# Attention with normed q and k, then a gelu MLP: the first two batches' steps issued in another order

## Chip, cores and metric

The kernel runs on one core of a Trainium2 chip. The metric is the device time of one execution in microseconds (us); the time given for a kernel is the median of its runs. The engines have in-order queues of their own: TensorE (PE; its weight loads are PEld), VectorE (DVE), ScalarE (ACT), GpSimd (POOL) and SyncE (SP, which only issues DMAs). Waits between them are semaphores, put in from the data that each instruction reads and writes.

## What is computed

Eight batches of attention with twelve heads, 448 tokens and a head size of 64, with q and k normed by their root mean square, and then two matrix products with a gelu between, on all 3584 tokens.

```python
def rmsnorm(x, g):
    rms = np.sqrt(np.mean(x * x, axis=-1, keepdims=True) + 1e-06)
    return x / rms * g
q_n, k_n = (rmsnorm(q, g_q), rmsnorm(k, g_k))
scores = scale * np.matmul(q_n, k_n.transpose(0, 1, 3, 2))
scores = scores - np.max(scores, axis=-1, keepdims=True)
attn = np.exp(scores)
attn = attn / (np.sum(attn, axis=-1, keepdims=True) + 1e-09)
x = np.matmul(attn, v)                 # heads side by side: 3584 x 768
h = x @ w_in                           # 768 x 2048
g = 0.5 * h * (1.0 + np.tanh(c * (h + 0.044715 * h * h * h)))
out = g @ w_out                        # 2048 x 768
```

## The kernel before

A batch is handled in three chunks of four heads (`c` = 0, 1, 2). The step names below carry an operand, a batch and a chunk: `q01` is q of batch 0, chunk 1. For each chunk of q and k the kernel loads the raw rows, squares them, totals the squares over the head (a row sum), takes the inverse root, multiplies (the norm), turns the result so that the head dimension lies on partitions, and puts it into `qT` or `kT`. The gains of q and k are multiplied into one column that scales `kT`. A constant `shift`, bounded from the gains, stands in for the row maximum in the exponential.

A *unit* (L325) is one seventh of a chunk's keys: TensorE makes scores in a pair of PSUM banks, ScalarE writes their exponentials to `ex`. There are 21 units in a batch, seven for each chunk. *Sums* are products of `ex` with ones (the softmax denominators), *products* are those with v. The denominators are transposed (`st`), inverted and spread (`rb`), and the products times `rb` are `xT`, the input of the MLP. The first layer (`hh` or a PSUM pair, L599) gives gelu's input, ScalarE writes `g`. The second layer takes two batches' tokens in quarters (L443): one *step* is four small matmuls, 32 steps make a group, and the group's last step copies its PSUM pair to `osb`. The second layer of batch 0 has 96 steps, which are mixed with the attention of batch 1.

Schedules are in the order of issue (`tc.manual_schedule()`): nothing reorders them. For batches 0 and 1 that order is a string, read by `first_two` (L814). From the first layer of batch 1 on, the loop over batches sets it. The words of the string:

- `y`, `z`, `w`: filler matmuls of zeros on TensorE (L272), 168 columns wide (`y`) or 448; `y` and `z` write the bank of `o`, `w` a buffer of the PSUM pool `ps_m`, which has two, taken in turn by turned tiles, roots, the sums of chunk 2 and `hh`. A number behind repeats the word.
- `L.q10`: a load of raw q or k on SP's queue (L125). The buffers rotate in fours, so a load waits for the square and the norm that read the buffer last.
- `sq`, `to`, `nm`, `tu`, `pu`: square (L170, L172), total (L177), norm (L279), turn (L297) and put (L306 to L310). `.A`, `.V`, `.P` name ScalarE, VectorE or GpSimd, `.h0`, `.h1` half the heads, `.t0`, `.t1` four and three of the seven token groups.
- `rA`, `rB`, `rC`, `r1`, `r2`, `rE`: inverse roots on ScalarE, a logarithm and exponentials (L202 to L221); `N1`: those of batch 1 by Newton steps on VectorE (L231 to L246). `eG`, `eE` load ScalarE's table for gelu or exp.
- `gp`, `gc`, `gm`, `sh`: the gains' product on GpSimd (L766), its transpose on VectorE (L772), the bound on TensorE (L777) and the shift on VectorE (L780, L784).
- `VV`, `Y`, `W`, `OO`: loads on GpSimd's DMA queue: v of a batch (L148, 672 KB as written), the first half of the columns of `win` in six parts (L738, 256 KB; `Y.10` is chunk 1, part 0), the second half in four (L728, 384 KB), and `wout` in two (L745, 1536 KB).
- `U`: a unit. `A`: an addition of exponentials on VectorE, which shortens the sums of batch 1. `s.c`, `x.c`: sums and products of a chunk, with a range of units behind. `t`, `r`, `q.c`: transpose of the denominators (L392), inverse and spread (L400, L401), and `xT` (L409, L415), all on VectorE.
- `m.i`: the first layer for a pair of column blocks (`e` the four parts of `xT` from chunks 0 and 1, `l` the last two), `h` half of one. `m.2.e` is the first, into `hh`.
- `a`, `d`: one second-layer step; the letter says whether ScalarE (`a`) or VectorE (`d`) makes the copy, and has an effect in the last step of a group alone.
- `dt`, `gn`: a transposing DMA on SP's queue (L315) in place of turn and put, and the gain for it. `PS`, `PT`: batch 1 begins; the small PSUM pools become two more pairs. `rel`: frees the spare raw buffers.

A sum or product of chunk `c` writes the same two banks `o` as the one before, so `x.0` waits for `t`, and `s.1` for `q.0`. The middle step of each second-layer group also puts a wait into SP's queue (L452).

Of the kernel before, what the change touches and what calls it, by code (L numbers as in the profile page):

```python
# [17 lines left out]
def kernel(  # L18
# [39 lines left out]
    gp = ctx.enter_context(tc.tile_pool(name="gp", bufs=1))  # L58
# [755 lines left out]
    def first_two(steps, m2):  # L814
# [3 lines left out]
        for step in steps.split():  # L818
# [78 lines left out]
            else:  # L897
# [10 lines left out]
                 "eE": lambda: nc.scalar.preload_act_table_set(EXP_SET)}[kind]()  # L908

    m2 = []  # L910
    first_two((
# [24 lines left out]
            )    , m2)  # L936
    begun = 2
    quads = ((3, 4), (5, 6))
    for b in range(1, B):
# [86 lines left out]
```

## Time and profile before

| | |
|---|---|
| Time, median of 3 runs | 393.82 us (393.76 to 394.06) |
| The profiled execution | 394.05 us, of which the span of the trace is 392.1 |
| TensorE busy | 384.0 us |
| ScalarE busy | 277.8 us |
| VectorE busy | 271.9 us |
| GpSimd busy | 125.8 us |
| DMA | 54.36 MB in 65770 packets |

Times in the profile count from the start of the span. A line of a timeline has start, length, engine, line, operation, what it writes and reads by the program's names, the shape, the count, and in brackets the engine's idle time before it with what ended that. Neighbouring instructions of one kind are merged. TensorE's matmuls overlap, and their ends are modelled. A DMA's landing is told as the time from its issue.

### The profile page before, as it was taken

The page shows a single profiled execution, that of the slowest core. Times are in us where ns is not written, and L with a number is a line of the kernel's source. Part 1 is how long each engine was busy: PE and PEld are TensorE (multiplying, and loading weights), DVE is VectorE, ACT ScalarE, POOL GpSimd, SP SyncE. Part 2 cuts the span into 40 slices and gives each one's busy share as a digit, 9 for nine tenths or more (in the row PEclk, how much of TensorE's full clock was granted, in tenths as well). Part 3 has the DMA queues.
Part 4 walks back from the last instruction along what each step waited for, and adds up shares of the span by engine and source line. Part 5 has one row for each costly group of instructions (what it writes and reads, how often), then busy time and mean ns, then how long its engine had stood idle before and what let it go on. Part 6 is the DMA issues. An engine that isn't in the chain of part 4 may idle for free.

```text
span 392.1 us, 12742 instructions
## 1 busy us (share of the span) xinstructions
PE 384.0 (98%) x5649; PEld 245.3 (63%) x5649; DVE 271.9 (69%) x424; ACT 277.8 (71%) x349; POOL 125.8 (32%) x105
## 2 busy tenths in 40 slices
PE   7989999999999999999999999999999999999996
PEld 6455567855676558865666557865566556875554
DVE  4999539996699357963599456982579613999743
ACT  6995489567996589857898479857899349873410
POOL 5995501863304540083301840054400900000000
PEclk9999999999999999999999999999999999999999
DMA  8999997899752969249651859239632621120024
GB/s 266 255 233 222 204 186 153 303 185 260 150 135 56 249 81 225 55 98 272 106 144 42 192 137 205 65 86 230 118 75 46 132 47 43 43 57 27 0 61 101
DMA packets 65770, 54.36 MB, mean 139 GB/s; under 512 B 37428, under 2 KB 60852, under 8 KB 65716
## 3 DMA queue, kind: packets, MB, share of 16 engines
q1 hardware_dynamic: 53200, 41.33, 41.9%
q0 software_dynamic: 12128, 11.80, 19.4%
q8 instruction: 44, 0.72, 0.8%
q10 hardware_dynamic: 388, 0.43, 0.3%
q14 instruction: 10, 0.08, 0.1%
HBM read 45.61 MB, written 11.01 MB: 144 GB/s over the span
## 4 chain that ended last, share of the span: by engine, by line
PE 91%; ACT 5%; DVE 1%; DMA 1%; issue 0%; POOL 0%; ACTq 0%
PE s L599 21%; PE t L443 19%; PE t L599 15%; PE s L443 12%; PE s L383 6%; ACT ex L338 4%; PE s L334 4%; PE t L334 3%; PE t L383 3%; PE s L529 2%; PE t L529 2%; PE o L383 1%; PE tp L297 1%; DMA rawq<-in_q_dram 1%; PE hh L599 1%
## 5 line engine op out<-in xcount | busy, mean ns | idle before, releaser
L599 PEld LDWEIGHTS <-win 128*128 128x128 bf16 x768 | 74.4, 98 | 70.8 <-issue 2.6
L443 PEld LDWEIGHTS <-g 64*64 64x64 bf16 x3072 | 98.0, 107 | 32.8 <-SPq L452 2.9
L338 ACT ACTIVATE ex<-s,shift 128x896 bf16<-128x896 f32 x101 | 97.8, 1011 | 4.5 <-PE s L334 2.7
L443 PE MATMUL t<-wout,g 64*64 64x384 bf16 x1792 | 90.4, 323 | 0.0
L599 PE MATMUL s<-xT,win 128*128 128x448 bf16 x438 | 88.3, 353 | 0.0
L177 DVE TENSOR_REDUCE ss<-sq 128x14 f32<-128x896 f32 (+3 forms) x45 | 44.4, 997 | 48.1 <-ACT sq L170 42.9
L338 ACT ACTIVATE ex<-t,shift 128x896 bf16<-128x896 f32 x67 | 66.4, 1014 | 5.8 <-PE t L334 3.0
L612 ACT ACTIVATE g<-s 128x896 bf16<-128x896 f32 (+1 forms) x41 | 34.0, 835 | 48.5 <-PE s L599 48.5
L599 PE MATMUL t<-xT,win 128*128 128x448 bf16 x318 | 64.7, 353 | 0.0
L443 PE MATMUL s<-wout,g 64*64 64x384 bf16 x1280 | 64.6, 323 | 0.1
L612 ACT ACTIVATE g<-t 128x896 bf16<-128x896 f32 (+1 forms) x30 | 24.8, 829 | 26.3 <-PE t L599 26.3
L334 PE MATMUL s<-qT,kT 64*64 64x448 bf16 x404 | 37.6, 353 | 2.0 <-ACT ex L338 1.5
L756 POOL COPY mark<-es 1x1 bf16<-1x1 bf16 x5 | 0.9, 177 | 116.0 <-DVE es L357 116.0
L279 POOL TENSOR_TENSOR nrmk<-rawk,rinv 128x896 bf16<-128x896 f32 (+1 forms) x21 | 34.5, 1647 | 5.4 <-DVE o L246 5.4
L279 POOL TENSOR_TENSOR nrmq<-rawq,rinv 128x896 bf16<-128x896 f32 (+1 forms) x21 | 34.5, 1643 | 4.2 <-ACT rinv L209 2.9
L334 PEld LDWEIGHTS <-kT 64*64 64x64 bf16 x672 | 23.7, 106 | 14.7 <-issue 6.3
L172 POOL TENSOR_TENSOR sq<-rawq 128x896 f32<-128x896 f32 (+1 forms) x9 | 13.6, 1516 | 54.1 <-DVE ss L177 28.2
L383 PEld LDWEIGHTS <-vb 64*64 64x64 bf16 x672 | 22.9, 107 | 8.1 <-issue 0.3
L401 DVE STREAM_TRANSPOSE rb<-rc 128x896 f32<-128x896 f32 x24 | 26.7, 1112 | 0.8
L334 PE MATMUL t<-qT,kT 64*64 64x448 bf16 x268 | 24.1, 351 | 0.3 <-ACT ex L338 0.2
L360 DVE TENSOR_TENSOR e<-ex 128x896 bf16<-128x896 bf16 x33 | 20.0, 606 | 6.2 <-ACT ex L338 6.2
L383 PE MATMUL s<-ex,vb 64*64 64x448 bf16 x420 | 22.8, 349 | 0.0
(123 smaller groups left out, 404.2 us busy)
## 6 DMA issues: line engine op xcount, KB each, us to landing
rawk<-in_k_dram SPq DMA_DIRECT2D x23, 448.0 KB, 5.6
out_dram<-osb SPq DMA_DIRECT2D x52, 192.0 KB, 3.1
rawq<-in_q_dram SPq DMA_DIRECT2D x22, 448.0 KB, 4.8
vb<-in_v_dram POOLq DMA_DIRECT2D x8, 672.0 KB, 7.2
wout<-in_moe_w_out_dram POOLq DMA_DIRECT2D x2, 1536.0 KB, 23.4
win<-in_moe_w_in_dram POOLq DMA_DIRECT2D x6, 256.0 KB, 11.2
win<-in_moe_w_in_dram POOLq DMA_DIRECT2D x4, 384.0 KB, 13.4
rawq<-in_q_dram SPq DMA_DIRECT2D x3, 224.0 KB, 3.9
```

Source lines behind the costliest of these rows:

```text
L172: eng.tensor_mul(sq, raw, raw)
L177: nc.vector.reduce_sum(sss[b][:, c, "qk".index(n), hs, ts], squares(b, c, n, hs, ts), axis=AX.X)
L279: eng.tensor_mul(nrms[n, b, c][:, ts].rearrange("p t a d -> p a t d"), raws[n, b, c][:, :, ts], root[:, :, ts].to_broadcast([P, 2, m, D]),)
L334: nc.tensor.matmul(sc[r * R:(r + 1) * R, a, :S], kT[rs, c, t, r], qT[b][rs, c, :, r], start=True, stop=True,)
L338: nc.scalar.activation(ex[:, t], sc[:, :, :S], AF.Exp, scale=scale, bias=shift)
L360: nc.vector.tensor_add(e2, ex[:, t - 1], ex[:, t])
L383: nc.tensor.matmul(o[r][a * D:(a + 1) * D], vb[b % 2][rs, 2 * c + a, i] if what else ones[rs], es[i][rs, a], start=(i == 0), stop=(i == n ...
L401: nc.vector.transpose(rb.rearrange("p r s -> p (r s)"), rc.to_broadcast([128, 2 * S // 32, 32]))
L443: done = nc.tensor.matmul(o[c * R:(c + 1) * R, n, :HD], g[rs, f, i * 128 + c * R:i * 128 + (c + 1) * R], wout[rs, f, half * HD:(half + 1) ...
L529: nc.tensor.matmul(o[:, lo:hi], g_of(qd, m, f), w_of(m, f)[:, lo:hi], start=start and f == 0, stop=f == nh - 1, skip_group_check=True,)
L599: nc.tensor.matmul(h[j][:, :S] if type(h) is list else h[:, j, :S], win[:, c, f * 128:(f + 1) * 128], xT[b][:, c], start=(c == 0), stop=(c ...
L612: nc.scalar.activation(g[:, 2 * i + lo:2 * i + js[-1] + 1, (b % 2) * S:(b % 2 + 1) * S], h[:, lo:js[-1] + 1, :S], AF.Gelu_apprx_tanh)
```

## The change

Only the string is changed: the same steps, but for two things, in another order. Sixteen of the 96 second-layer steps have the letter `a` instead of `d`, and the square `sq.k21.h1` is ScalarE's instead of GpSimd's. Of the fillers, `z1` stands ahead of the 48 `y`, and `z6`, `w5` and two single `z` stand ahead of or among the turns of `q00`; formerly `w5` and most `z` stood among the units of chunk 0. `gp` stands ahead of the first GpSimd norm. On GpSimd's DMA queue the order was `VV.0`, `Y.00`, `Y.01`, `Y.10`, `Y.11`, `Y.20`, `Y.21`, `W.10` to `W.13`, `OO.0`, `OO.1`, `VV.1`; it is now `VV.0`, `W.13`, `Y.11`, `Y.01`, `Y.21`, `Y.00`, `Y.10`, `Y.20`, `W.12`, `W.11`, `W.10`, `VV.1`, `OO.0`, `OO.1`. `nm.k01.P.t1` stands ahead of `sq.k02.P`. In batch 1 units, steps, additions, loads, squares and totals are mixed in another way.

```diff
--- before.py
+++ after.py
@@ -908,32 +908,24 @@
                  "eE": lambda: nc.scalar.preload_act_table_set(EXP_SET)}[kind]()
 
     m2 = []
-    first_two((
-                "y48 sq.q00.A.h0 to.q00.h0 sq.q00.A.h1 z3 to.q00.h1 sq.k00.A.t0 "
-                "to.k00.t0 sq.k00.P.t1 rA nm.q00.P.t1 gp rB nm.q00.V.t0 L.q10 "
-                "sq.q01.A tu.q00.t0 tu.q00.t1 nm.k00.V.t0 pu.q00.A VV.0 gc z1 "
-                "to.k00.t1 rC tu.k00.t0 pu.k00.V.t0 gm sh z1 U2 nm.k00.V.t1 w5 "
-                "sq.k01.P sq.k02.P tu.k00.t1 to.q01 to.k01 U r1 sq.q02.P U "
-                "pu.k00.V.t1 nm.k01.V.t0 z1 nm.q01.V to.q02 z6 U z1 U to.k02 s.0.01 "
-                "U s.0.13 nm.k01.P.t1 tu.q01 s.0.34 pu.q01.V tu.k01 Y.00 Y.01 Y.10 "
-                "r2 s.0.47 pu.k01.V.t0 U L.k10 U Y.11 Y.20 nm.q02.P Y.21 t sq.q10.P "
-                "sq.k10.P W.10 W.11 nm.k02.V.t0 nm.k02.V.t1 W.12 W.13 pu.k01.V.t1 "
-                "z4 z1 r U x.0.01 L.q12 sq.q12.P x.0.12 OO.0 x.0.23 OO.1 rel U "
-                "tu.q02 tu.k02 pu.k02.V.t1 pu.k02.V.t0 U pu.q02.V x.0.37 q.0 to.q10 "
-                "L.k12 L.q11 to.k10 U3 s.1.05 VV.1 U s.1.57 U2 t s.2.01 x.1.03 U "
-                "x.1.35 U x.1.57 r q.1 U eG s.2.16 x.2.01 sq.k12.P x.2.13 to.q12 "
-                "s.2.67 x.2.37 t r q.2 to.k12 sq.q11.A L.k11 m.2.e sq.k11.P to.q11 "
-                "to.k11 N1 nm.k11.P nm.k12.P m.0.e m.1.e m.0.l m.1.l nm.q12.P "
-                "nm.q10.V nm.k10.V m.2.l m.3 m.4 nm.q11.V tu.q10 pu.q10.V m.5 "
-                "tu.k10 m.6 tu.q11 pu.q11.V pu.k10.V h.7.0 h.7.1 PS a eE tu.k11 "
-                "pu.k11.V U A PT a6 U a3 U2 a2 d4 dt.k12 d dt.q12 U2 d7 A U A3 d U "
-                "d A2 d U d9 A U d4 a s.0 A U A t r a6 d L.q20 L.k20 L.q21 gn.12 U2 "
-                "A2 U A L.k21 sq.q20.P sq.k20.P d sq.q21.P.h0 sq.k21.P.h0 L.q22 "
-                "L.k22 sq.q21.P.h1 d4 x.0 U A U d5 q.0 s.1 t d2 A2 U2 d2 "
-                "sq.k21.P.h1 d3 A d to.k20 d5 U2 r to.q21.h0 to.q20 x.1 U a d a "
-                "to.k21.h0 A2 q.1 A to.q21.h1 L.q30 L.k30 a2 x.2 a4 A s.2 sq.q22.A "
-                "sq.k22.P t d9 r d2 to.k21.h1 rE d2 VV.2 d2 a eG q.2 m.0.e m.1.e"
-            )    , m2)
+    first_two(("z1 y48 sq.q00.A.h0 sq.k00.P.t1 z3 to.q00.h0 gp sq.q00.A.h1 to.q00.h1 sq.k00.A.t0 to.k00.t0 rA "
+               "z6 nm.q00.V.t0 rB nm.k00.V.t0 w5 sq.q01.A tu.q00.t0 z1 z1 nm.q00.P.t1 tu.q00.t1 pu.q00.A "
+               "to.k00.t1 tu.k00.t0 L.q10 VV.0 gc rC z1 pu.k00.V.t0 gm sh to.q01 U2 nm.k00.V.t1 sq.k01.P W.13 U "
+               "to.k01 r1 U tu.k00.t1 pu.k00.V.t1 nm.k01.V.t0 U2 nm.q01.V sq.q02.P nm.k01.P.t1 tu.k01 sq.k02.P "
+               "U Y.11 to.q02 Y.01 s.0.01 tu.q01 Y.21 s.0.13 s.0.34 pu.k01.V.t0 to.k02 s.0.47 r2 nm.q02.P "
+               "pu.q01.V U2 t Y.00 L.k10 sq.q10.P sq.k10.P Y.10 nm.k02.V.t1 Y.20 z1 nm.k02.V.t0 W.12 z4 W.11 "
+               "pu.k01.V.t1 r U W.10 x.0.01 VV.1 x.0.12 x.0.23 U L.q12 tu.k02 pu.k02.V.t1 tu.q02 U pu.q02.V "
+               "pu.k02.V.t0 x.0.37 U sq.q12.P U2 q.0 s.1.05 OO.0 to.q10 U s.1.57 U to.k10 U t s.2.01 x.1.03 U "
+               "x.1.35 x.1.57 U L.k12 sq.k12.P r U eG L.k11 q.1 rel s.2.16 OO.1 x.2.01 x.2.13 L.q11 to.q12 "
+               "s.2.67 x.2.37 t sq.k11.P r q.2 m.2.e m.0.e sq.q11.A to.q11 to.k11 to.k12 N1 nm.q10.V nm.k10.V "
+               "m.1.e m.0.l m.1.l m.2.l m.3 m.4 tu.q10 nm.q12.P m.5 m.6 tu.k10 pu.k10.V h.7.0 h.7.1 PS d "
+               "pu.q10.V eE nm.q11.V tu.q11 nm.k11.P tu.k11 pu.q11.V U pu.k11.V PT d a A a3 U dt.q12 a d2 U2 d "
+               "a d2 nm.k12.P d a d U2 d A dt.k12 a d a A U d2 A a A d A2 a3 U a L.q20 A U a2 d3 a2 d a U d3 a2 "
+               "U A s.0 t a2 d U d A L.q21 a A L.k20 sq.k20.P d U gn.12 A2 U a A L.k21 L.k22 d L.q22 "
+               "sq.k21.P.h0 d2 L.q30 sq.q21.P.h0 r x.0 U a d U q.0 a d a3 s.1 a2 d t a sq.q20.P A2 U d2 A r a "
+               "sq.k21.A.h1 d2 U to.k20 a d4 U2 a A2 sq.q22.A d2 A d U to.q21.h0 L.k30 A a3 x.1 q.1 to.k21.h1 d "
+               "x.2 s.2 to.k21.h0 VV.2 t d a to.q20 d8 a sq.q21.P.h1 to.q21.h1 a d a sq.k22.P rE eG a r q.2 "
+               "m.0.e m.1.e"), m2)
     begun = 2
     quads = ((3, 4), (5, 6))
     for b in range(1, B):
```

## Prediction

> **What bounds the kernel now.** I read the page first, then stretches of the span, then each engine's timeline up to 36 us.
>
> ```profile
> span 392.1 us, 12742 instructions
> PE 384.0 (98%) x5649; PEld 245.3 (63%) x5649; DVE 271.9 (69%) x424; ACT 277.8 (71%) x349; POOL 125.8 (32%) x105
> ```
>
> TensorE is busy for 98% of the span, but part of that is filler (`y`, `z`, `w`: products of zeros). The next view gives busy time by stretch: PE, PEld, DVE, ACT, POOL, then clock and DMA.
>
> ```profile
> 9.88:31.17 21.29, 19.28 (x277) 10.41 (x274) 19.98 (x31) 20.42 (x27) 19.98 (x22) 1.00 1.08 245
> 32.30:52.00 19.70, 19.70 (x125) 10.60 (x121) 13.61 (x26) 8.07 (x12) 8.20 (x5) 1.00 1.26 206
> 52.00:80.00 28.00, 27.61 (x604) 20.67 (x601) 22.08 (x35) 22.03 (x24) 9.47 (x8) 1.00 0.91 204
> ```
>
> From 9.88 to 31.17 us ScalarE works 20.42 of 21.29 us: it leaves 0.87 us. From 32.30 to 80, past the end of what the change reorders, TensorE has no gap but 0.4 us between 52 and 80. So whatever batch 0's front loses or wins by 32.3 us is passed on whole, and behind it there is 0.4 us to win. ScalarE's timeline of the front:
>
> ```profile
> 7.65 0.95 ACT L170 ACTIVATE g<-rawq 128x896 f32<-128x896 f32 x1 [0.49 <-DMA rawq<-in_q_dram]
> 8.51 0.89 ACT L308 COPY qT<-tp 128x896 bf16<-128x896 bf16 x1
> 9.88 2.80 ACT L338 ACTIVATE ex<-s,shift 128x896 bf16<-128x896 f32 x3
> 13.15 3.68 ACT L338 ACTIVATE ex<-s,shift 128x896 bf16<-128x896 f32 x4
> 17.45 0.18 ACT L221 ACTIVATE root<-lg 128x14 f32<-128x14 f32 x1 [0.27 <-DVE qT L310]
> 18.23 12.92 ACT L338 ACTIVATE ex<-s,shift 128x896 bf16<-128x896 f32 x14 [0.47 <-PE s L334]
> ```
>
> The 21 exponentials (3, 4, 14) run nearly back to back, 12.92/14 = 0.92 us each. So the front's end is set by when the first begins, 9.88 us. That needs `qT` (8.51 + 0.89 = 9.40), the first scores, and the shift. TensorE up to there, and where the second layer's first half-batch begins:
>
> ```profile
> 1.17 5.79 PE L272 MATMUL o<-zeros 128*128 128x168 bf16 x51 [1.17 <-DVE zeros L84]
> 7.45 0.56 PE L297 MATMUL tp<-ident,nrmq 128*128 128x128 bf16 x7 [0.49 <-DVE nrmq L279]
> 8.37 0.41 PE L777 MATMUL s<-gprod,rows 32*128 32x32 f32 x4
> 9.44 0.57 PE L334 MATMUL s<-qT,kT 64*64 64x448 bf16 x8 [0.36 <-DVE shift L784]
> 9.95 1.12 PE L272 MATMUL w<-zeros 128*128 128x448 bf16 x5
> 12.15 1.50 PE L272 MATMUL o<-zeros 128*128 128x448 bf16 x7
> 32.32 1.68 PE L599 MATMUL hh<-xT,win 128*128 128x448 bf16 x8
> ```
>
> Ends are modelled; the next matmul issues before them. A `z` or `w` costs (1.50 - 1.12)/2 = 0.19 us of issue, and the last one's tail is 1.12 - 5 x 0.19 = 0.17. The opening filler (48 `y`, 3 `z`) issues until 6.96 - 0.17 = 6.80 us (rounded); after its end TensorE waits 0.49 us for the normed q. Its own slack ahead of the first turn is about half a microsecond.
>
> **The change, part by part.**
>
> *Fillers, the largest term.* Their number stays (48 `y`, 18 `z`, 5 `w`), but ahead of `tu.q00.t0` now stand one more `z` at the very front, `z6` and `w5`; two more split the seven turns. The first writes the `o` bank that holds nothing yet, `w` a fresh PSUM buffer, so neither waits; TensorE takes them in order. Eleven cost 11 x 0.19 = 2.09 us. The front `z` runs while TensorE is slow:
>
> ```profile
> 1.10:4.37 3.27, 3.20 (x24) 1.00 0.77 231
> 4.37:6.20 1.83, 1.83 (x27) 1.00 0.98 249
> ```
>
> Of the `y`, 24 fall in the first 3.27 us (0.14 each), 27 touch the next 1.83 (0.07 each), though the granted-clock column says 1.00 in both. If the slow stretch lasts a fixed time, the `z` pushes `y` into the fast part and costs 0.19 in the end; if a fixed number of matmuls, 0.14 x 448/168 = 0.37. I take the smaller, since the matmuls on both sides of the step are alike and only time has passed. [...] This trace alone fits both.
>
> So the first turn issues at 6.80 + 2.28 = 9.08 us instead of 7.45; seven turns to their end 0.56, two `z` between 0.38: done at 10.02. `pu.q00.A` starts at about 10.07 instead of 8.51: **+1.56 us**. In the old order it also waited for `sq.q01.A` to end, so 1.56 is what is left of TensorE's longer delay.
>
> *The gain product.* `gp` moves ahead of `nm.q00.P.t1` on POOL.
>
> ```profile
> 6.68 0.83 POOL L279 TENSOR_TENSOR nrmq<-rawq,rinv 128x384 bf16<-128x384 f32 x1 [0.18 <-ACT s L221]
> 7.47 0.57 POOL L766 TENSOR_TENSOR gprod<-grow 64x32 f32<-64x32 f32 x2
> ```
>
> ```profile
> 9.27 0.15 DVE L784 TENSOR_SCALAR shift<-shift 128x1 f32<-128x1 f32 x1
> ```
>
> The norm waits for the product's 0.57 less the 0.18 that POOL idled: it ends 0.4 later, near 7.9 us, covered by the fillers, which run to 9.08. Without that cover it would cost 0.4. The bound (`gm`) comes behind the turns of `q00` and half of `k00` and one `z` and ends near 10.75; the shift ended 0.64 behind it before (8.78 to 9.42), so by 11.4 at the latest. The first scores issue at 10.96 + 0.04 = 11.0 and the first exponential starts at 11.44, again +1.56, with the shift just in time.
>
> *Totals and norms of chunks 1 and 2.* `to.q01` now stands ahead of `nm.k00.V.t1`; it fills VectorE's wait of 0.41 us for the root of `rC` and delays `tu.k00.t1`, which only unit 5 needs, by then behind two exponentials: nothing. The root step `r1` is still between exponentials 3 and 4. Ahead of `r2` stands `pu.k01.V.t0` (0.48, below), which moves the root, bound to `pu.q01.V`, by 0.4; exponential 8 formerly waited for that same `kT`, and now for `pu.q01.V`: about equal. I take 0.1, bounds 0 and 0.5.
>
> ```profile
> 9.84 0.56 DVE L279 TENSOR_TENSOR nrmk<-rawk,o 128x384 bf16<-128x384 f32 x1 [0.41 <-ACT o L221]
> 16.74 0.61 DVE L310 COPY qT<-tp 128x896 bf16<-128x896 bf16 x1
> 17.27 0.48 DVE L306 TENSOR_SCALAR kT<-tp,gcols 128x512 bf16<-128x512 bf16 x1
> ```
>
> Units, sums and products of batch 0 keep their order but for one pair; each waits for the same releases 1.6 us later. `m.2.e` thus starts at 32.32 + 1.6 to 1.7 = 34.0.
>
> *POOL and the weight loads.* `nm.k01.P.t1` now stands ahead of `sq.k02.P`, so that square waits for the roots of `r1`, which ScalarE ends as it takes up exponential 4 (13.15 before, 14.7 now). Behind it are six of the ten loads of `win`; only `W.13` is issued early (10.6 us).
>
> ```profile
> 20.71 1.70 POOL L172 TENSOR_TENSOR sq<-rawq 128x896 f32<-128x896 f32 x1
> ```
>
> ```profile
> L738 POOL DMA_DIRECT2D win<-in_moe_w_in_dram x1: 642/642/642, 20.1 to 20.1; - x1
> ...
> DMA to landing us min/median/max: 13.3/13.3/13.3
> ```
>
> ```profile
> L728 POOL DMA_DIRECT2D win<-in_moe_w_in_dram x1: 665/665/665, 24.0 to 24.0; - x1
> ...
> DMA to landing us min/median/max: 11.6/11.6/11.6
> ```
>
> Adding POOL's durations (1.7 a square or norm, 0.64 an issue), `Y.11` is issued at 17.3 instead of `Y.00` at 15.4, and `Y.10`, the last part `m.2.e` needs, at 25.4. The queue lands parts in order: six of 256 KB by 20.1 + 13.3 = 33.4 us, the seventh, of 384 KB, by 35.6. `Y.10` now has `W.13` (384) and four `Y` ahead, with itself 1664 KB against 1536 and 1920: 33.4 + 2.2 x 128/384 = 34.1. The third matmul needs it at 34.4. No wait on this estimate; it can cost 1.2 if it lands like the seventh part. I take 0.1. `W.10` to `W.12` land as late as the old last part, under 43 us, when `m.4` comes. `OO.0` landed at 28.1 + 20.3 = 48.4 (below) and now lies behind `VV.1` too, 672 KB, at 2.2 us for 384 KB 3.8 us: there by 52.2, needed at 51.74 + 1.6 = 53.3, covered by 1.1.
>
> ```profile
> L745 POOL DMA_DIRECT2D wout<-in_moe_w_out_dram x1: 1211/1211/1211, 28.1 to 28.1; - x1
> ...
> DMA to landing us min/median/max: 20.3/20.3/20.3
> ```
>
> ```profile
> 51.74 0.36 PE L443 MATMUL s<-wout,g 64*64 64x384 bf16 x4
> ```
>
> SP's loads of batch 1 keep their order but for `k11` ahead of `q11`, and go 1.5 to 2 us later as their buffers come free; `to.q11` to `to.k12` wait for `q.2` anyway.
>
> *Batch 1.* Sixteen `d` become `a`. Only steps 32, 64 and 96 copy anything, and these are `d`, `d`, `a` before and after: nothing. `sq.k21.h1` moves from POOL to ScalarE, about half a square, in a stretch where ScalarE idles (22.03 of 28): nothing; uncovered 0.6. Two tiles are now turned behind `h.7` instead of one, which adds no work; but VectorE must do `pu.k10.V`, `pu.q10.V` and `nm.q11.V` (0.68 + 0.62 + 1.08 = 2.4 us) while TensorE does `h.7` (2.3 us of issue) and one step: 0.1, bounds 0 and 0.3.
>
> ```profile
> 43.66 1.08 DVE L279 TENSOR_TENSOR nrmq<-rawq,o 128x896 bf16<-128x896 f32 x1
> 50.12 0.68 DVE L306 TENSOR_SCALAR kT<-tp,gcols 128x896 bf16<-128x896 bf16 x1
> ```
>
> ```profile
> 49.38 2.43 PE L599 MATMUL s<-xT,win 128*128 128x448 bf16 x12
> ```
>
> Units stand with fewer steps between them at first (the sixth behind 16 steps, formerly 17), more later. The gap of 0.4 in 52 to 80 may go or double: 0, bounds -0.4 and +0.5. The loads of batch 2 leave earlier, and `dt.q12` no longer stands behind SP's wait for step 16.
>
> **Sum.** 1.56 + 0.1 + 0.1 + 0.1 + 0 = 1.9 us. The profiled execution took 394.05 us (span 392.1 and 1.95 around it), 0.23 above the median 393.82. So 394.05 + 1.86 = 395.9, and as a median **395.7 us**.
>
> **Rivals.**
>
> *The weights come late.* POOL's queue slides by more than counted and `Y.10` lands with the old seventh part or later. For it: DMA share 1.08 in the front. Against: the same bytes lie ahead within 128 KB. +1.2: 396.9.
>
> *TensorE slows again.* The `w5` at 9.95 us and the seven `z` at 12.15 are gone from a thin stretch; from 11 to 16.5 us TensorE would work under half the time. If it falls to its opening pace until rewarmed (3.2 us at half), 1.6 us of work is lost, partly in its 2.0 us of gaps: +1.2, 396.9. Against: no pause there exceeds 1 us. [...]
>
> *Batch 1 stalls.* Pairs of PSUM run short where units stand close: one exponential's length, 0.92 + 0.1: 396.7.
>
> *Not slower.* The fillers ahead of the first turn would have to fit into TensorE's 0.49 us there, that is cost 0.045 each, not 0.19. Then `pu.q00.A` stays at 8.51 behind `sq.q01.A`, the front keeps its times, and at best batch 1 wins its 0.4: 393.82 - 0.4 = 393.4. The turning point is `pu.q00.A` at 8.5. ScalarE can't win it back otherwise: its whole slack is 0.87, less than 1.56.
>
> **How the numbers follow.** Forecast 0.60 (394.9 to 396.4), late weights 0.13, slow TensorE 0.08, batch 1 stalls 0.10, not slower 0.09. The range 394.8 to 397.2 takes in all but the last and the tails. A measurement can tell about 0.2% (0.8 us) from no change: faster 0.06, same 0.04, slower 0.90.
>
> **What would show it.** Right: eleven fillers ahead of the first turn, that turn near 9.1 us, `pu.q00.A` at 10.1, first exponential at 11.4, `hh` at 34.0, no wait in TensorE from there to 54. Wrong: the first exponential before 10.5; `hh` over 34.5, with a wait for `win`; transposes at 0.11 instead of 0.055 apart around 16 us; gaps of TensorE over 0.9 us between 54 and 82.

## Result and the profile after

| | before | changed |
|---|---|---|
| Time, median of 6 runs each, side by side | 393.94 us (393.69 to 395.29) | 397.84 us (396.64 to 399.18) |
| Ratio | | 1.0092, 95% interval 1.0067 to 1.0117 |
| Profiled execution | 394.05 us, span 392.1 | 399.18 us, span 397.4 |

Slower, as forecast, but by 3.9 us and not by 1.9. Ratios, here and below, compare runs taken side by side and leave out the slow ones (two of the ten of fillers_back, one of the ten of shorter_opening), so a ratio need not be the quotient of two medians. The page of the changed kernel:

```profile
span 397.4 us, 12737 instructions
PE 385.7 (97%) x5649; PEld 246.9 (62%) x5649; DVE 274.2 (69%) x424; ACT 278.6 (70%) x350; POOL 125.0 (31%) x104
```

Stretches of the changed kernel: stretch, its length, busy time of PE, PEld, DVE, ACT, POOL, then TensorE's granted clock and DMA. The first two are the opening, the next three single out the clock, the last three answer to those shown of before:

```profile
1.10:4.37 3.27, 3.20 (x22) 2.98 (x23) 0.29 (x6) 1.76 (x2) 1.26 (x3) 1.00 0.75 245
4.37:7.24 2.87, 2.87 (x24) 2.87 (x22) 2.64 (x5) 2.12 (x8) 1.74 (x4) 1.00 0.97 303
10.65:14.03 3.38, 2.22 (x29) 1.40 (x27) 2.36 (x6) 2.56 (x5) 2.40 (x3) 1.00 1.18 228
14.03:17.44 3.41, 1.57 (x20) 0.58 (x16) 2.79 (x4) 3.38 (x7) 1.24 (x2) 1.00 1.17 215
17.44:20.85 3.41, 3.41 (x37) 1.94 (x38) 3.26 (x5) 2.75 (x5) 3.01 (x4) 0.50 0.85 250
12.75:34.00 21.25, 16.58 (x244) 9.44 (x243) 19.32 (x31) 19.60 (x27) 17.33 (x19) 0.92 1.07 230
36.19:55.22 19.03, 19.03 (x113) 10.07 (x110) 13.00 (x25) 7.90 (x11) 6.92 (x5) 1.00 1.27 202
55.22:83.95 28.73, 27.86 (x611) 20.94 (x611) 22.74 (x36) 22.50 (x25) 7.02 (x7) 1.00 0.91 203
```

Two things are new. From 4.37 to 7.24 us TensorE issues 24 matmuls in 2.87 us (0.12 each), the slow pace; in the profile of before the fast pace began near 4.4. The trace's own record of the clock begins only there, at 4.47 us before and at 7.20 in the changed kernel; ahead of it there is no entry, and the column shows 1.00. And from 17.44 to 20.85 the granted clock is 0.50, behind a stretch in which TensorE was busy 1.57 of 3.41 us. In before it was busy nearly throughout there, and the clock stayed up:

```profile
11.30:14.71 3.41, 3.13 (x26) 1.07 (x22) 2.97 (x5) 3.38 (x7) 3.34 (x3) 1.00 1.20 208
14.71:18.12 3.41, 3.28 (x54) 1.70 (x51) 3.27 (x6) 2.76 (x6) 3.41 (x6) 1.00 1.05 273
```

ScalarE's timeline of the changed kernel:

```profile
7.73 0.95 ACT L170 ACTIVATE g<-rawq 128x896 f32<-128x896 f32 x1 [0.95 <-DMA rawq<-in_q_dram]
11.36 0.91 ACT L308 COPY qT<-tp 128x896 bf16<-128x896 bf16 x1 [2.68 <-PE tp L297]
12.75 2.80 ACT L338 ACTIVATE ex<-s,shift 128x896 bf16<-128x896 f32 x3
16.03 3.84 ACT L338 ACTIVATE ex<-s,shift 128x896 bf16<-128x896 f32 x4
21.96 1.91 ACT L338 ACTIVATE ex<-s,shift 128x896 bf16<-128x896 f32 x2 [0.84 <-PE s L334]
```

`pu.q00.A` now waits 2.68 us for the turn. The first exponential is 12.75 - 9.88 = 2.87 us late, and the way from the first to the eighth takes 9.21 us instead of 8.35. TensorE's timeline of the changed kernel:

```profile
10.39 0.39 PE L297 MATMUL tp<-ident,nrmq 128*128 128x128 bf16 x4
...
17.38 0.91 PE L297 MATMUL tp<-ident,nrmk 128*128 128x128 bf16 x7
...
36.19 1.11 PE L599 MATMUL hh<-xT,win 128*128 128x448 bf16 x5
...
55.22 0.36 PE L443 MATMUL s<-wout,g 64*64 64x384 bf16 x4
...
70.35 0.38 PE L334 MATMUL t<-qT,kT 64*64 64x448 bf16 x4 [0.57 <-DVE kT L321]
74.55 0.38 PE L334 MATMUL t<-qT,kT 64*64 64x448 bf16 x4 [0.23 <-DVE st L392]
...
115.40 0.33 PE L443 MATMUL t<-wout,g 64*64 64x384 bf16 x3
116.76 0.51 PE L443 MATMUL t<-wout,g 64*64 64x384 bf16 x5 [1.02 <-issue]
```

Seven turns of the slow clock take 0.91 us (0.56 before). Neither `hh` nor the first step waits for weights. At 116.76, in the middle of a step, TensorE stands for 1.02 us with no releaser.

Where the 5.2 us of span went, from the marks of the two timelines: 2.87 to the first exponential; 0.86 from there to the eighth; 0.14 to `hh`; nothing to the first unit of batch 1; 0.17 in batch 1; 1.2 behind it, most of it the pause of 1.02.

### The profile page after: what moved, and what is told of

The parts are those of the page before. It is cut to its first block, busy times and chain, and to the rows that moved or that the text cites. A ratio compares the mean times of both kernels' runs of the same rounds, so it can differ in the third digit from the quotient of the medians.

```text
span 397.4 us, 12737 instructions
## 1 busy us (share of the span) xinstructions
PE 385.7 (97%) x5649; PEld 246.9 (62%) x5649; DVE 274.2 (69%) x424; ACT 278.6 (70%) x350; POOL 125.0 (31%) x104
## 4 chain that ended last, share of the span: by engine, by line
PE 90%; ACT 5%; DVE 3%; issue 1%; DVEq 0%
PE s L599 20%; PE t L443 20%; PE t L599 16%; PE s L443 9%; PE s L383 6%; PE s L334 4%; ACT ex L338 4%; PE t L334 3%; PE o L272 2%; PE s L529 2%; PE t L529 2%; PE t L383 2%; PE o L383 1%; PE tp L297 1%; DVE st L392 1%
## 5 line engine op out<-in xcount | busy, mean ns | idle before, releaser
L338 ACT ACTIVATE ex<-s,shift 128x896 bf16<-128x896 f32 x103 | 100.0, 1013 | 5.5 <-PE s L334 3.3
L443 PE MATMUL t<-wout,g 64*64 64x384 bf16 x1920 | 96.9, 323 | 1.0 <-issue 1.0
L599 PE MATMUL s<-xT,win 128*128 128x448 bf16 x426 | 85.7, 353 | 0.0
L177 DVE TENSOR_REDUCE ss<-sq 128x14 f32<-128x896 f32 (+3 forms) x45 | 44.2, 997 | 47.3 <-ACT sq L170 41.1
L338 ACT ACTIVATE ex<-t,shift 128x896 bf16<-128x896 f32 x65 | 64.4, 1018 | 6.9 <-PE t L334 4.1
L599 PE MATMUL t<-xT,win 128*128 128x448 bf16 x330 | 66.9, 353 | 0.0
L612 ACT ACTIVATE g<-s 128x896 bf16<-128x896 f32 (+1 forms) x40 | 33.1, 832 | 46.9 <-PE s L599 46.9
L443 PE MATMUL s<-wout,g 64*64 64x384 bf16 x1152 | 58.8, 323 | 0.0
L612 ACT ACTIVATE g<-t 128x896 bf16<-128x896 f32 (+1 forms) x31 | 25.7, 832 | 26.7 <-PE t L599 26.7
L172 POOL TENSOR_TENSOR sq<-rawk 128x896 f32<-128x896 f32 (+2 forms) x11 | 17.3, 1574 | 31.5 <-DMA rawk<-in_k_dram 20.5
L383 PE MATMUL s<-ex,vb 64*64 64x448 bf16 x448 | 24.3, 349 | 0.0
```

The lines of the kernel that those rows point to most:

```text
L172: eng.tensor_mul(sq, raw, raw)
L177: nc.vector.reduce_sum(sss[b][:, c, "qk".index(n), hs, ts], squares(b, c, n, hs, ts), axis=AX.X)
L338: nc.scalar.activation(ex[:, t], sc[:, :, :S], AF.Exp, scale=scale, bias=shift)
L383: nc.tensor.matmul(o[r][a * D:(a + 1) * D], vb[b % 2][rs, 2 * c + a, i] if what else ones[rs], es[i][rs, a], start=(i == 0), stop=(i == n ...
L443: done = nc.tensor.matmul(o[c * R:(c + 1) * R, n, :HD], g[rs, f, i * 128 + c * R:i * 128 + (c + 1) * R], wout[rs, f, half * HD:(half + 1) ...
L599: nc.tensor.matmul(h[j][:, :S] if type(h) is list else h[:, j, :S], win[:, c, f * 128:(f + 1) * 128], xT[b][:, c], start=(c == 0), stop=(c ...
```

## Experiments

Marks of the profiles (us), read off the timelines: end of the opening's slow pace, first turn, first and eighth exponential and their distance, `hh`, first second-layer step, and the stretch of batch 1 from its first unit to `m.0` of the next batch.

| profile | opening | turn | exp 1 | exp 8 | 1 to 8 | `hh` | step 1 | batch 1 |
|---|---|---|---|---|---|---|---|---|
| before | 4.49 | 7.45 | 9.88 | 18.23 | 8.35 | 32.32 | 51.74 | 27.38 |
| changed | 7.24 | 10.39 | 12.75 | 21.96 | 9.21 | 36.19 | 55.22 | 27.55 |
| changed_again | 5.44 | 9.56 | 11.92 | 22.25 | 10.33 | 36.30 | 55.33 | 26.41 |
| no_fillers | 4.92 | 7.27 | 10.43 | 19.79 | 9.36 | 34.02 | 55.73 | 26.42 |
| fillers_back | 5.74 | 7.39 | 10.99 | 19.34 | 8.35 | 33.35 | 52.89 | 26.66 |
| fillers_both | 6.98 | 10.30 | 12.65 | 21.00 | 8.35 | 35.01 | 56.47 | 27.41 |
| before_with_fillers_ahead | 6.42 | 10.04 | 12.39 | 21.87 | 9.48 | 36.03 | 55.45 | 27.38 |
| front_before_back_after | 6.61 | 7.85 | 10.03 | 18.39 | 8.36 | 32.48 | 51.51 | 26.41 |
| front_after_back_before | 6.67 | 10.12 | 12.48 | 21.64 | 9.16 | 35.87 | 55.30 | 27.38 |
| fillers_and_weights_back | 4.35 | 7.23 | 10.59 | 18.93 | 8.34 | 32.94 | 51.97 | 26.41 |
| half_the_fillers_back | 5.44 | 9.54 | 11.90 | 20.25 | 8.35 | 34.15 | 55.65 | 27.44 |
| shorter_opening | other fillers | 8.38 | 10.79 | 21.06 | 10.27 | 35.17 | 54.96 | 26.41 |
| new_back_again | 5.06 | 7.12 | 10.28 | 18.64 | 8.36 | 32.74 | 51.77 | 26.41 |
| new_back_later_v | 3.95 | 7.31 | 11.11 | 20.87 | 9.76 | 34.97 | 54.00 | 27.63 |
| weights_back | 4.88 | 9.28 | 11.63 | 21.96 | 10.33 | 36.02 | 55.05 | 27.61 |
| weights_back_half_fillers | 6.81 | 10.18 | 12.54 | 20.89 | 8.35 | 34.79 | 53.97 | 26.59 |
| three_undone | other fillers | 8.07 | 10.94 | 19.29 | 8.35 | 33.18 | 52.21 | 26.41 |

### The fillers

**no_fillers**: the fillers put ahead are left out.

```diff
-z1 y48 sq.q00.A.h0
+y48 sq.q00.A.h0
...
-rA z6 nm.q00.V.t0 rB nm.k00.V.t0 w5 sq.q01.A tu.q00.t0 z1 z1 nm.q00.P.t1
+rA nm.q00.V.t0 rB nm.k00.V.t0 sq.q01.A tu.q00.t0 nm.q00.P.t1
```

> The changed kernel without the 14 fillers ahead of and among the first turns (z1, z6, w5, two single z). Theory (fillers ahead of the first turn plus a clock that falls in the thin stretch behind them): the first exponential comes back to 9.6 to 9.9 us, the granted clock still falls to half once before hh, since nothing fills 11 to 17 us; about 394.8, 0.9 over the kernel before. Rival (the order of norms, totals and weight loads costs the time): first exponential at 9.9 but hh at 34 or later and 396 or more.

Measured: 396.22 us, ratio 1.0064 (1.0035 to 1.0094). The first exponential is 2.3 us earlier than in the changed profile, and the time is only 1.6 lower. Its stretches:

```profile
8.36:11.77 3.41, 1.64 (x22) 0.89 (x20) 2.79 (x7) 3.31 (x6) 2.62 (x3) 1.00 1.06 320
11.77:15.18 3.41, 2.15 (x19) 0.68 (x14) 2.38 (x4) 3.38 (x7) 3.15 (x4) 0.50 1.19 199
15.18:18.60 3.42, 3.42 (x34) 1.89 (x34) 3.27 (x5) 2.63 (x4) 2.95 (x4) 0.50 1.17 246
```

The clock is at half for two stretches, of 3.41 and 3.42 us, and a wait of 1.80 us for the norm of `q10` is new:

```profile
39.73 0.95 ACT L170 ACTIVATE g<-rawq 128x896 f32<-128x896 f32 x1 [5.58 <-DMA rawq<-in_q_dram]
...
48.03 0.56 PE L297 MATMUL tp<-ident,nrmq 128*128 128x128 bf16 x7 [1.80 <-DVE nrmq L279]
```

The first line is the square of `q11`. All roots of batch 1 are taken in one go behind it, and its raw rows, the last of batch 1 to be loaded in the new order, landed 17.4 us after their issue, in the changed profile 10.0. So leaving out fillers takes away one loss, keeps the other and uncovers a third. The time of 396.22 and `hh` at 34.02 are what the rival named, not the 394.8 expected, and the first exponential missed its 9.6 to 9.9: the time of this run does not tell theory and rival apart.

**fillers_back**: no_fillers with as many fillers in the front as before had, at before's places.

```diff
-gm sh to.q01 U2 nm.k00.V.t1
+gm sh to.q01 U2 z5 nm.k00.V.t1
...
-nm.k01.V.t0 U2 nm.q01.V
+nm.k01.V.t0 z8 U z1 U nm.q01.V
```

> The changed kernel with those fillers put where the kernel before has them (z5 behind the first two units, eight z ahead of unit 5, one ahead of unit 6). Theory: first exponential at 9.6 to 9.9, no fall of the granted clock in the front, hh at 32.4, 393.9 to 394.3, within 0.1% of before. Rival (order of norms, totals, weights or batch 1): 396 or more with hh beyond 33.5.

Measured: 395.66 us, ratio 1.0020 (0.9999 to 1.0041), over the 393.9 to 394.3 expected. The clock stays up, 8.35 us from the first to the eighth exponential, but the first comes at 10.99 instead of 9.6 to 9.9. GpSimd's and TensorE's timelines tell why: the second part of `q00` is turned only behind GpSimd's norm, and that stands behind the moved gain product (0.56 us) and a square whose raw rows landed at 6.90 us, in before at 5.67:

```profile
7.69 0.56 POOL L766 TENSOR_TENSOR gprod<-grow 64x32 f32<-64x32 f32 x2
...
9.22 0.34 PE L297 MATMUL tp<-ident,nrmq 128*128 128x128 bf16 x3 [1.45 <-POOL nrmq L279]
```

TensorE's timeline also shows a wait that the changed kernel did not have:

```profile
52.89 0.36 PE L443 MATMUL s<-wout,g 64*64 64x384 bf16 x4 [0.44 <-DMA wout<-in_moe_w_out_dram]
```

**fillers_both**: the changed kernel, its fillers ahead left in place, with the fourteen `z` of fillers_back besides.

> The changed kernel with its fillers ahead kept, and fourteen more z in the thin stretch among units 3 to 6. Theory: first exponential as late as in the changed kernel (11.4 to 12.8), but no fall of the clock, transposes 0.055 us apart throughout, nine tenths of a microsecond less between the first and the eighth exponential (8.35 us instead of 9.2): 1 us below the changed kernel, 396.0 to 396.8. Rival (the fall has another cause): it falls as before and the time is 397.8 or more.

Measured: 397.62 us, ratio 1.0085 (1.0060 to 1.0110): no gain, where 1 us was expected, though the clock stays up and `hh` comes at 35.01. TensorE's timeline tells where it went:

```profile
56.47 0.36 PE L443 MATMUL s<-wout,g 64*64 64x384 bf16 x4 [2.36 <-DMA wout<-in_moe_w_out_dram]
```

**before_with_fillers_ahead**: the kernel before with the fillers at the changed places, nothing else.

```diff
-y48 sq.q00.A.h0
+z1 y48 sq.q00.A.h0
...
-nm.q00.V.t0 L.q10 sq.q01.A tu.q00.t0 tu.q00.t1
+nm.q00.V.t0 z6 w5 L.q10 sq.q01.A tu.q00.t0 z1 z1 tu.q00.t1
...
-U2 nm.k00.V.t1 w5 sq.k01.P
+U2 nm.k00.V.t1 sq.k01.P
...
-nm.k01.V.t0 z1 nm.q01.V to.q02 z6 U z1 U to.k02
+nm.k01.V.t0 nm.q01.V to.q02 U U to.k02
```

> The kernel before with only the fillers moved as in the change (one z ahead of the y, z6 and w5 ahead of the first turn, two z among the turns; none among units 3 to 6). Theory: first exponential at 11.4 to 12.8, clock falls once in the front, 396.4 to 397.5. Rival (fillers cost nothing, the order of the other steps does): 393.9.

Measured: 397.67 us, ratio 1.0080 (1.0063 to 1.0097). Moving the fillers alone costs what the whole change costs, 0.2 us more than the top of what I expected, and its profile has both marks: first exponential at 12.39, and the clock at half from 16.70:

```profile
13.29:16.70 3.41, 1.17 (x13) 0.41 (x13) 2.97 (x5) 3.38 (x8) 2.14 (x3) 1.00 1.07 223
16.70:20.11 3.41, 3.40 (x31) 1.82 (x30) 2.75 (x4) 3.00 (x4) 2.96 (x5) 0.50 0.66 105
```

**shorter_opening**: 20 `y` for 48 in the changed kernel.

> The changed kernel with 20 y at the front instead of 48; all else as changed, z1, z6, w5 and the two single z ahead of or among the first turns included. Theory (fillers ahead of the first turn are what the front loses, and an opening whose slow pace lasts longer than in the profile of before makes it worse): 28 y are 2.0 us at the fast pace and 3.9 us at the slow one, so the first turn is set by the normed q at 7.9 to 8.8 us instead of 9.6 to 10.4, the first exponential comes at 10.0 to 11.0 instead of 11.9 to 12.75; the clock's fall in the thin stretch stays. Time 396.4 (395.8 to 397.0). Rival (the gain product ahead of the first GpSimd norm, or the load of q01, sets the front, and the fillers are cover): first exponential at 11.4 or later, time 397.4 or more.

Measured: 396.94 us, ratio 1.0058 (1.0032 to 1.0085); first exponential at 10.79. In the changed kernel the fillers are thus the bound of the front's start, not the moved gain product and not `q01`. The clock falls as before (two stretches, behind a busy share of 1.47/3.41), and TensorE waits 0.59 us for the norm of `q10`, as in no_fillers.

**half_the_fillers_back**: seven of the fourteen `z`.

```diff
-U2 nm.k00.V.t1 sq.k01.P W.13
+U2 z2 nm.k00.V.t1 sq.k01.P W.13
...
-nm.k01.V.t0 U2 nm.q01.V
+nm.k01.V.t0 z3 U z2 U nm.q01.V
```

> The changed kernel with seven more z in the thin stretch (two ahead of nm.k00.V.t1, three ahead of unit 5, two ahead of unit 6), half of what fillers_both had. Theory (the clock falls when TensorE's busy share of one stretch of 3.413 us, on a raster of its own, is too low: in the profiles so far a half-clock stretch followed shares of 0.34 to 0.48 and never shares of 0.61 or more): seven z of 0.19 us are 1.3 us, so the thin stretch's share goes from about 0.45 to 0.65 to 0.8 and the clock stays up; from the first exponential to the eighth 8.35 us, not 9.2 to 10.3. Time 396.9 (396.2 to 397.4), because part of what is won is met by the wait for wout behind VV.1 at the first second-layer step, as in fillers_both. Rival 1 (all fourteen are needed, TensorE must be fed without pause): the fall stays, 397.8. Rival 2 (the clock's fall lies on no path): 8.35 us, but a time within 0.3 of 397.8 and no new wait for wout.

Measured: 398.55 us, ratio 1.0095 (1.0065 to 1.0125). The first half held (8.35 us, busy share 2.46/3.41 = 0.72, no fall in the front), the time, expected at 396.2 to 397.4, did not. Stretches of this kernel:

```profile
12.26:15.67 3.41, 2.46 (x22) 0.93 (x20) 2.80 (x5) 3.38 (x7) 2.03 (x3) 1.00 1.19 178
...
53.22:56.63 3.41, 1.00 (x18) 0.81 (x18) 0.09 (x2) 1.83 (x2) 0.00 (x0) 1.00 1.31 194
56.63:60.05 3.42, 3.42 (x45) 1.87 (x46) 1.13 (x2) 1.44 (x2) 0.00 (x0) 0.50 1.30 203
```

At the first second-layer step it waits 2.41 us for `wout`, and behind the stretch with that wait, busy 1.00 of 3.41 us, the clock falls in turn. Its time is thus no measure of the first fall; the weights had to be put right first.

### The weights

**fillers_and_weights_back**: fillers_back with the loads on GpSimd's queue in before's order, at the changed places.

```diff
-VV.0 W.13 Y.11 Y.01 Y.21 Y.00 Y.10 Y.20 W.12 W.11 W.10 VV.1 OO.0 OO.1
+VV.0 Y.00 Y.01 Y.10 Y.11 Y.20 Y.21 W.10 W.11 W.12 W.13 OO.0 OO.1 VV.1
```

> The run with the fillers put back, and also the loads of win, wout and v in the order of the kernel before, at the places where the changed kernel issues its fourteen loads. Theory (wout's first half behind v of batch 1 lands too late once the front is early): no wait for wout at the first second-layer step, 0.5 to 1 us below the run with the fillers alone, 394.2 to 395.0. Rival (that wait is chance of the DMAs' rates): a wait of the same 0.4 to 0.9 us is there again.

Measured: 394.70 us, ratio 0.9989 (0.9962 to 1.0017). `OO.0` lands at 48.15 us instead of 52.85, and no step waits for it.

**weights_back**: the changed kernel with that order, all fillers as changed.

> The changed kernel with the loads on GpSimd's queue in before's order (OO.0 and OO.1 ahead of VV.1), at the changed places; all fillers as changed. Theory: wout lands before 52 us, so no wait for it can come; but in the changed kernel the late front had hidden it, so the time stays: 397.6 (396.9 to 398.3); a half-clock stretch in the front again, first exponential 11.9 to 12.8. Rival (the new order of the loads is itself the loss): 396.8 or less.

Measured: 396.66 us, ratio 1.0052 (1.0023 to 1.0080), under the 396.9 at which the theory's range began and within the rival's, 396.8 or less. The interval overlaps that of the changed kernel, and neither profile of the changed kernel has a wait for weights, so a cost of the order of loads within the changed kernel is likely in some executions but not shown.

**weights_back_half_fillers**: weights_back with the seven `z` of half_the_fillers_back.

> weights_back with seven z in the thin stretch, as in half_the_fillers_back. Theory (the clock's fall lies on the path; in half_the_fillers_back and fillers_both the wait for wout took its place): no half-clock stretch before 300 us, 8.35 us from the first to the eighth exponential, no wait for wout; 0.9 to 2.0 us below weights_back: 396.3 (395.6 to 397.0). Rival (the fall is on no path): within 0.4 of weights_back.

Measured: 395.44 us, ratio 1.0017 (0.9997 to 1.0036), 1.2 us below weights_back, measured beside it; nine of its ten runs lie below the lowest of the six of weights_back. No fall in the front, 8.35 us against 10.33. With no late weights to take its place, the fall lies on the path.

**three_undone**: the same with 20 `y`.

> weights_back_half_fillers with 20 y in place of 48: the three losses undone at once, with the fillers ahead of the first turns, the moved gain product and the new batch 1 left as they are. Theory (those three are the loss): first exponential 10.2 to 11.0, eighth 8.35 us behind it, no wait for wout, 394.5 (393.8 to 395.3), that is 3.3 below the changed kernel. Rival (a further loss in batch 0's front, or behind it, is not among them): 395.8 or more.

Measured: 393.47 us, ratio 0.9987 (0.9960 to 1.0013), beside 394.29 for before: lower than the 394.5 expected, not to be told from before. ScalarE's timeline:

```profile
10.94 2.80 ACT L338 ACTIVATE ex<-s,shift 128x896 bf16<-128x896 f32 x3
...
14.21 3.68 ACT L338 ACTIVATE ex<-s,shift 128x896 bf16<-128x896 f32 x4
...
19.29 1.01 ACT L338 ACTIVATE ex<-s,shift 128x896 bf16<-128x896 f32 x1
```

With the three undone the loss is gone. What is left of it at `hh`, 33.18 - 32.32 = 0.86 us, is made up again: 0.4 by the first step, 0.97 in batch 1. Of that rest the fillers that still stand ahead are one part; another is GpSimd's norm behind the moved gain product, for which TensorE waits 0.34 us ahead of the second part of `q00`.

### The two halves, and batch 1

**front_before_back_after** has before's words up to `N1`, then the changed ones; **front_after_back_before** the reverse.

```diff
-z1 y48 sq.q00.A.h0 sq.k00.P.t1 z3 to.q00.h0 gp
...
-s.2.67 x.2.37 t sq.k11.P r q.2 m.2.e m.0.e sq.q11.A to.q11 to.k11 to.k12 N1
+y48 sq.q00.A.h0 to.q00.h0 sq.q00.A.h1 z3 to.q00.h1
...
+s.2.67 x.2.37 t r q.2 to.k12 sq.q11.A L.k11 m.2.e sq.k11.P to.q11 to.k11 N1 m.0.e
 nm.q10.V nm.k10.V m.1.e
```

> The words of the kernel before up to the Newton roots of batch 1, then those of the changed kernel (units, steps, loads and squares of batch 1 mixed its way). Theory: the time lies in the front, so 394.2 to 394.8, with 0.2 to 0.6 us of new TensorE gaps between 52 and 85 us, one at the unit behind the gain gn.12. Rival (batch 1's order costs a third of it): 395.5 or more.

Measured: 393.99 us, ratio 0.9979 (0.9953 to 1.0005), a little under the 394.2 to 394.8 expected and without the new gaps. Batch 1 in before, then in this run:

```profile
52.53:79.91 27.38, 26.99 (x594) 20.18 (x593) 21.99 (x35) 21.52 (x23) 9.47 (x8) 1.00 0.90 205
...
52.68:79.09 26.41, 26.35 (x595) 20.43 (x593) 21.09 (x35) 21.26 (x24) 6.94 (x7) 1.00 1.05 233
```

> The changed kernel's words up to the Newton roots of batch 1, then those of the kernel before. Theory: 397 to 397.8, with the clock fall in the front and hh at 35 to 36.2. Rival: 396 or less.

Measured: 397.44 us, ratio 1.0063 (1.0039 to 1.0086), stretch 27.38 us. The loss is in the front, and the new batch 1 is 0.97 us shorter than before's 27.38.

**new_back_again**: front_before_back_after word for word.

> front_before_back_after word for word once more, on the same chip and beside the same runs of before. Theory (the new order of batch 1 is worth about 1.0 us in the stretch from its first unit to m.0 of the next batch, and gives 0 to 0.5 us back at 111 us): 393.6 (393.2 to 394.1), first exponential by 10.1 us, that stretch 26.4 us instead of 27.4, ratio 0.998. Rival (the shorter stretch was one execution's): ratio 1.000, stretch 27.2 or more.

Measured: 393.98 us, ratio 0.9987 (0.9967 to 1.0007), stretch 26.41 us. The shorter stretch repeats; a gain in time is not shown.

**changed_again**: the changed kernel word for word, one run.

> The changed kernel once more, word for word, for the length of TensorE's slow opening. Theory (it ends by a window of time that runs free of the program, so its length differs between executions): the fast pace begins somewhere between 4.4 and 7.6 us, not at 7.24 as before, and the first exponential moves by half of the difference; the clock falls once in the front again. Rival (the z at the very front makes the opening long): the fast pace begins between 6.5 and 7.3 again.

Measured: 397.3 us, one run. The opening ends at 5.44 instead of 7.24, the clock is at half for two stretches instead of one, and batch 1 takes 26.41 us. What differs in batch 1 is one operation on VectorE. The timeline of the changed profile:

```profile
68.28 1.77 POOL L172 TENSOR_TENSOR sq<-rawk 128x896 f32<-128x896 f32 x1 [17.77 <-DMA rawk<-in_k_dram]
...
68.42 1.87 DVE L321 TENSOR_SCALAR kT<-kT,gcols 128x896 bf16<-128x896 bf16 x1
```

The same two in the timeline of changed_again:

```profile
68.53 0.45 DVE L321 TENSOR_SCALAR kT<-kT,gcols 128x896 bf16<-128x896 bf16 x1
...
68.96 2.09 POOL L172 TENSOR_TENSOR sq<-rawk 128x896 f32<-128x896 f32 x1 [18.04 <-DMA rawk<-in_k_dram]
```

The gain `gn.12` takes 0.45 us, but 1.87 when the square of `k20` has begun 0.14 us before it: it ends just behind the square. TensorE's unit waits (0.57, then 0.23 us, above), and the stretch is 1.1 us longer. The square starts as its raw data land, so a DMA's landing time decides whether the two meet. weights_back has the same (1.93 us). In new_back_later_v and fillers_both the addition of exponentials is hit instead, 2.11 and 2.10 us for 0.62. These four profiles have batch 1 at 27.41 to 27.63 us; the nine others with the new order and with no fall of the clock there have it at 26.41 to 26.66. No experiment moved the square on purpose, so the link rests on these profiles.

**new_back_later_v**:

```diff
-            side.append((0, lambda: load_v(b + 2, 0, HP)))
+            side.append((6 if b == 1 else 0, lambda: load_v(b + 2, 0, HP)))
```

> front_before_back_after, with v of batch 3 loaded at unit 16 of batch 2 instead of unit 0. In four of the six profiles with the new back, TensorE stood still for 0.16 to 1.02 us at the same place of its queue (the 1499th or 1501st matmul), waiting for no semaphore, and went on within 0.1 us of the landing of the output stored while that load of v (672 KB as written) was under way. Theory (that pause is bound to the transfers queued beside the load of v): no pause there, and the output stored near 105 us lands in under 5 us instead of 6.5; time 0.0 to 0.5 below new_back_again. Rival (the pause has another cause): a pause of 0.2 to 1.0 us may stand at the same place still; time as new_back_again.

Measured: 393.60 us, ratio 0.9987 (0.9967 to 1.0008), no pause. But the load was issued 3.7 us behind batch 2's first unit, against 3.2 in new_back_again: the edit hardly moved it, so it tested nothing of the pause. The profile has something else, in before's own front:

```profile
7.35:10.77 3.42, 1.92 (x21) 1.31 (x25) 1.82 (x6) 1.94 (x3) 3.20 (x6) 1.00 0.99 348
10.77:14.18 3.41, 3.41 (x24) 1.16 (x16) 2.95 (x4) 2.09 (x3) 2.72 (x3) 0.50 0.86 169
```

Its opening was the shortest (3.95 us), and the second stretch behind it held only 1.92 us of work, as TensorE waited 0.60 and 0.94 us for the two parts of the norm of `q00`: the clock fell, and the eighth exponential came at 20.87. So before's own order can fall too.

## Why the forecast fell short, step by step

Two steps failed: the term for the fillers ahead, 1.56 us, was 1.7 to 1.95, and the fall of TensorE's clock, worth about 1.2, was left out of the sum.

**Fillers ahead: the step was right, its size was not.** I took the opening's slow stretch from one execution, 3.2 us, and weighed only whether it is a time or a count. It is neither a fixed count nor a fixed time. In the profile of before 24 matmuls fall in it up to 4.37 us, in the changed one 46 up to 7.24 (22, then 24); and in the 15 profiles with 48 `y` it ends between 3.95 and 7.24 us, at 5.7 in the mean. The trace's record of the clock has the stretch at half from 17.44 us in the changed kernel as one entry of 3.413 us. Where the clock falls later in the front, it does so a whole number of such stretches behind the end of the opening: 17.44 - 7.24 = 10.20, 15.71 - 5.44 = 10.27, 11.77 - 4.92 = 6.85, 16.88 - 6.67 = 10.21, 16.70 - 6.42 = 10.28 (three, three, two, three, three). So in these five the rise and the fall lie on one raster of 3.41 us. That the kernel's start lies elsewhere on it in each execution is my reading of the 15 ends, which are 3.29 us apart at most, less than one step; no run shows it by itself. The profile of before, with 4.49, was a short one. The 0.19 for the `z` at the very front rested on a fixed time; no run moved that `z` alone. In the eight profiles with 48 `y` and the fillers ahead, the first exponential follows the opening on a line: 11.63 at 4.88, 11.92 at 5.44, 12.39 at 6.42, 12.65 at 6.98, 12.75 at 7.24, about half a us for one. At 4.49 that line gives 11.45; I had forecast 11.44. Their mean is 12.28, and that of the four profiles with before's front is 10.33: 1.95 apart instead of 1.56, and 2.87 in the one profiled. Part of the 1.95 is luck, for the eight openings average 6.23 us and the four 5.03; at the mean of all fifteen, 5.67, the line gives 12.01, which is 1.7 above before. So I put the term at 1.7 to 1.95. Before has slack that hides part of a long opening (first exponential at 10.03 behind one of 6.61), the changed kernel has none.

**The clock's fall: a rival at 0.08 that happened.** All seven profiles with no fillers in the thin stretch have it in the front, and one of the ten with fillers there. I argued against it that no pause there exceeds 1 us. That a fall takes a longer pause was my assumption, which no row showed. The pauses in the changed profile were that short (0.92 us at most), and the clock fell all the same. Nor did every long one bring it down: the stretch of no_fillers from 45.91 us holds a pause of 1.80 us, that of fillers_both from 54.79 most of one of 2.36, and behind neither the clock fell. What tells most of the falls is the busy share of one stretch. Behind shares of 0.34 to 0.48 (1.57/3.41 = 0.46 in the changed profile) and once 0.56 the clock fell; behind 0.61 or more it never did, in any of the 17 profiles. Behind a share of 0.29 (the wait for `wout` in half_the_fillers_back) it fell too. But the two stretches with the long pauses, with shares of 0.47 and 0.51, were followed by none, so the bound is not sharp, or the share is not all that counts. A half-clock stretch ended behind one busy throughout; one busy 0.63 to 0.85 was followed by a second. From the first to the eighth exponential that costs 0.8 to 1.4 us for one stretch and 1.0 to 2.0 for two; I had priced 1.2, and weights_back_half_fillers against weights_back gives 1.2 as a time. The fall and its price were in the forecast as a rival; the sum held none of it, and the chance was wrong.

With these two, 395.7 + (0.1 to 0.4) + 1.2 = 397.0 to 397.3. The last 0.5 to 0.8 up to 397.84 I can't assign: falls of two stretches, waits for `wout` in executions that were not profiled, the meeting of `gn.12` with the square, and the pause below are candidates.

**Totals, norms, `hh`.** From the eighth exponential to `hh` 14.23 us, 14.09 before: the 0.1 I gave. In the changed kernel the gain product cost nothing, under the cover of the fillers that I had named; without that cover TensorE waited 0.38 (no_fillers), 1.45 (fillers_back) and 0.34 us (three_undone) for the norm behind it. I had priced 0.4 there, and taken the landing of `k00`'s raw rows from one execution; it lies between 5.34 and 6.98 us in the 17 profiles.

**Weights.** `Y.10` landed at 34.79 us, forecast 34.1, and `hh` did not wait. `OO.0` landed at 51.95, forecast 52.2, and was needed at 55.22. My cover of 1.1 us held only because the front was later still; with the front or the clock mended it landed at 52.85 to 56.43, and TensorE waited up to 2.4 us. I had priced the landing from one execution and given it no range. The same holds for the loads of batch 1, of which I said that nothing waits for them: true in the changed profile, but in no_fillers and shorter_opening the late `q11` held TensorE for 1.80 and 0.59 us.

**Batch 1.** I gave 0, within -0.4 to +0.5. Against before the order is worth -0.97 in most profiles in which no such operation was hit, and +0.17 in the one of the changed kernel, where `gn.12` met the square. I never asked what the earlier start of batch 2's squares would run beside. What the 0.97 consists of I have not settled: the gaps of 0.4 us that I saw in before are gone, the rest is closer issue of the steps.

**The signs I named.** No wait in TensorE from `hh` to 54 us: right. First turn 10.39 for 9.1, `pu.q00.A` 11.36 for 10.1, first exponential 12.75 for 11.4, `hh` 36.19 for 34.0: late by the opening and the fall. Transposes at 0.11 us instead of 0.055 apart near 16 us was named as a sign against me, and it came at 17.38.

## What to carry to other kernels

A duration that depends on how an execution happens to begin, like TensorE's slow opening here (its end from 3.95 to 7.24 us), needs a range from several profiles, and the slack ahead of the first real work has to cover its long end. Before moving fillers out of a thin stretch, add up TensorE's busy share there over every 3.4 us, instead of looking only for the longest pause: here the clock fell behind shares of 0.29 to 0.56 of such a stretch, though not behind each of them, and behind none of 0.61 or more. And mend causes together before judging one: with the fall cured alone, the late `wout` took its place (waits of 2.36 and 2.41 us in fillers_both and half_the_fillers_back).

## What else the hardware showed

Where the gain (alone 0.45 us) or the addition of exponentials (alone 0.62) on VectorE met GpSimd's square of 128x896 f32 (alone 1.68) in the profiles named here, one of the two took longer. In the changed kernel, weights_back and new_back_later_v VectorE's took 1.87, 1.93 and 2.11 us, to 0.2 to 0.5 us behind the square's end; in changed_again, where VectorE's started first, the square took 2.09. The order of starts does not decide alone: in half_the_fillers_back the addition started 0.02 us behind the square, at 70.36, and took 0.62, and the square took 2.18. Row sums of squares (L177) that began beside such a square took 1.08 to 1.09 us (at 12.45 and 105.21 us in the changed kernel), as elsewhere.

The pause at 116.76 us stands at one place of TensorE's queue, its 1499th or 1501st matmul, in 5 of the 14 profiles with the new batch 1 and in none of the 3 with the old, and lasts 0.16 to 1.02 us. In the DMA view of the changed kernel from 114 to 116 us stands one packet of a queue of its own:

```profile
q8 instruction: 1, 0.02, 2.8%
```

In all five, such a packet of 16 KB (16384 bytes each in the traces of before and of the changed kernel) ends 1.3 to 1.6 us before TensorE goes on, while the load of v of batch 3 is under way; in before it ended 1.2 us ahead of the same place, as TensorE just came there. The trace names this queue for instructions; that the pause, up to 1.02 us, is a wait for this packet is no more than my guess from these times. In the changed kernel the packet ends at 115.16 us and TensorE goes on at 116.76. No experiment here moved the packet, so no run shows what causes the pause.
